# Three head edits in a fused recurrent-scan and gated-MLP kernel: the first loads on one hardware queue, ScalarE copies tile 0's transposes whole, tile 3's statistics ahead of tile 2's norm

## The chip, the cores and the metric

The kernel runs on one core of a Trainium2 chip. The metric is the device time of one execution in microseconds, the median of several runs. A core has five instruction streams that run side by side and meet at semaphores: PE (TensorE, matrix products), DVE (VectorE), ACT (ScalarE), POOL (GpSimd) and SP, which here does nothing but issue DMA transfers. ACT and POOL can issue transfers too; all of them run on the core's 16 DMA engines. Each stream takes its instructions strictly in order.

## The reference

`x` has 2048 rows (tokens) of 448 features. Everything is in bfloat16.

```python
xn = _layernorm(x, axis=-1)                      # (x - mean) / sqrt(var + 1e-5)

# A: a diagonal complex recurrence over the tokens (P = 448 states)
dt = exp(log_dt);  Lam_bar = exp(dt * Lam)
B_bar = ((Lam_bar - 1.0) / Lam)[:, None] * Bmat
Bu = einsum("bld,pd->blp", xn, B_bar)
h_t = Lam_bar * h_(t-1) + Bu_t                   # 2048 steps
s = 2.0 * einsum("blp,dp->bld", hseq, Cmat).real + xn * Dskip

# B: a gated MLP, F = 1792
g = einsum("bsd,df->bsf", xn, w_gate);  u = einsum("bsd,df->bsf", xn, w_up)
g = silu(einsum("bsf,fd->bsd", sigmoid(g) * u, w_down))

return x + s * g
```

## The kernel before, in words

The 2048 rows are 16 tiles of 128 rows; four tiles make a chunk, and four chunks are worked on in turn. For each chunk the normed rows are transposed so that features lie on the partitions (`xnT`, four blocks of 128 features by 512 rows). PE then makes the products with the gate and up weights in seven units each (`g0` to `g6`, `u0` to `u6`, two blocks of 128 outputs per unit), the products with B (`b_phase`), and for an earlier chunk the down product and the product with C. DVE runs the recurrence as a scan after a rotation by tables of sines and cosines (`ssm_pair`, `ssm_stack`), and combines gate and up (`gu_evac`). Chunks 1 to 3 are transposed by DMA; chunk 0 is transposed on PE, since nothing else is there for PE to do.

Products of 448 features are cut into halves of 64 rows, which run beside each other on the two halves of PE's rows: `ph_mm` issues six products of a unit, `z_mm` two more. A unit is `ph_mm`, `z_mm`, `ph_mm`, 14 instructions in 7 pairs.

**The planner.** The code doesn't issue instructions at once. Every operation is added to a plan with its engine, an estimated cost, the keys it reads and writes, and for transfers an assumed landing time (`land=`). `solve` (line 139) computes latest and earliest times and picks an order for each engine; `emit` writes the instructions in that order. PE's order is always that of the program text. DVE's and ACT's order is that of the text while `pl.seq` is true, that is, in the head of the kernel (lines 1094 to 1172); after it the planner is free to choose, so a changed cost or landing time in the head can move DVE and ACT instructions much later in the kernel. Transfers of SP and ACT share eight completion semaphores in turn: the ninth waits for the first to land.

**The head, chunk 0** (lines 388 to 421 and 1093 to 1168). The loads: SP's queue takes x tile 0, x tile 1, the gate weights in six pieces (`load_w`, three blocks of outputs by two halves of the features), x tiles 4 to 7 in two loads, the up weights. ACT's queue takes the row of the recurrence's real parts (`load_p("ACT", 2)`), x tile 2, and x tile 3. POOL's queue takes the two other rows, `log_dt` and the imaginary parts. A first table for ACT's square root is loaded in between.

PE starts with ten products of constants of 512 columns (`warm_mm`). Statistics of tiles 0, 1 and 3 are made on DVE (`bn` then `aggr`), those of tile 2 on ACT (`act_mean`, `act_var`); then a root on ACT (`root`, `act_root`), a reciprocal and the norm on DVE (`recip`, `norm`), in the order of lines 1098 to 1149. Tile 0 is transposed by four 128x128 transposes into two PSUM banks (`pe_transpose`), DVE copies one bank and ACT the other to `xnT`. The three rows of the recurrence are turned into columns by small products in the same place (`columns`; ACT copies them with `copy_pv`). Five more products of constants (`fill`) follow. Tiles 1, 2 and 3 are transposed in eight pieces of 64 rows (`row_transpose`); tile 1's result is copied whole by ACT (`pair_copy`), tiles 2 and 3 in two halves by ACT and DVE (`row_copy`; both halves of tile 3 by DVE).

The gate products of chunk 0 go tile by tile as the tiles arrive: units 0 and 1 of one tile at a time (`units[t]`, 128 columns), unit 2 for two tiles at a time (`pairs`, 256 columns); `front` is a unit's first eight instructions, `back` its last six. The order on PE is: tile 0's transposes, columns, fill, tile 1's transposes, `front` and `back` of `units[0]`, `front` of `units[1]`, tile 2's transposes, `back` of `units[1]`, `front` of `pairs[0]`, `front` of `units[2]`, tile 3's transposes, the rest. The head's last product is followed by unit 3, the first one of 512 columns.

Of the kernel before, what the change touches and what calls it, by code (L numbers as in the profile page):

```python
# [21 lines left out]
P = 128  # L22
# [225 lines left out]
def kernel(  # L248
# [27 lines left out]
    def flat(t, *dims):  # L276
        if len(dims) == 1:
            return t
        names = "abcd"[:len(dims)]
        kw = {n: v for n, v in zip(names[1:], dims[1:])}  # L280
        return t.rearrange("p (" + " ".join(names) + ") -> p " + " ".join(names), **kw)
# [81 lines left out]
    def load_x(t0, n, q="SP", r=(), rate=230e3, land=0.0):  # L363
        load(q, [("x", t) for t in range(t0, t0 + n)], n * P * D * 2,
             x_all[:, t0:t0 + n, :], x_src[:, t0:t0 + n, :], r=r, rate=rate, land=land)
# [3 lines left out]
    def load_w(eng, k, b, part, r=(), land=0.0):  # L369
        m0, m1 = BLK[k][b]  # L370
        c0, c1, r0 = m0 * 2 * P, m1 * 2 * P, (0, 192)[part]
        load(eng, [("w", k, m, part) for m in range(m0, m1)], 4 * P * (c1 - c0), wgt[k][:, 2 * part:2 * part + 2, c0:c1],
             wsrc[k][r0:r0 + 2 * P, c0:c1].rearrange("(s p) f -> p s f", p=P), cost=0.65, r=r, rate=400e3, land=land)
# [17 lines left out]
    def load_p(eng, k, r=()):  # L391
        load(eng, ("vrow", k), D * 2, vrow[k:k + 1, :], (A_log_dt, A_Lambda_im, A_Lambda_re)[k].unsqueeze(0), cost=0.75 if eng == "POOL" else 0.45, r=r)
    load_x(0, 1, "SP")
    load_p("ACT", 2)
    load_x(1, 1, "SP", land=3.6)
    load_x(2, 1, "ACT", land=3.8)
    add("ACT", 0.05, lambda: A.preload_act_table_set("sqrt_and_others"), w=["sqrttab"], lat=1.3, chain=True)
    load_x(3, 1, "ACT", land=4.3)
    load_w("SP", "g", 0, 0, land=5.2)
    load_w("SP", "g", 0, 1, land=5.6)  # L400
    load_p("POOL", 0)
    load_p("POOL", 1)
    add("POOL", 0.15, lambda: G.memset(ident[:], 0.0), w=["ident"], chain=True)
    add("POOL", 0.4, lambda: G.affine_select(out=ident[:], in_=ident[:], compare_op=ALU.not_equal, fill=1.0, base=0,
                                             pattern=[[-1, P]], channel_multiplier=1), r=["ident"], w=["ident"], chain=True)
# [1 line left out]
    load_w("SP", "g", 1, 1, land=7.2)  # L407
    load_w("SP", "g", 2, 0, land=8.4)
    load_w("SP", "g", 2, 1, land=9.6)
    load_x(4, 2, land=10.4)  # L410
    load_x(6, 2, land=11.1)
    add("POOL", 0.1, lambda: G.memset(halfc[:], 0.5), w=["consts"])
    add("POOL", 0.1, lambda: G.memset(negc[:], -1.0), r=["consts"], w=["consts"])
    add("POOL", 0.1, lambda: G.memset(expc[:], math.e), w=["expc"])
# [60 lines left out]
    def act_var(t):  # L475
        add("ACT", 0.7, lambda: A.activation(junk[:], x_all[:, t, :], ACT.Square, bias=nmf[:, t, :], accum_out=sqf[:, t, :]),
            r=[("x", t), ("nf", t)], w=[("mv", t), "junk"])
# [29 lines left out]
    def xkey(t):  # L507
        return t if t < TPC else TPC + t % NXN
# [30 lines left out]
        touch(3)  # L539
        return a  # L540

    def pe_transpose(t, keys, banks):
        o, js = xbuf(t), slice(t * P, t * P + P)
        for i, (key, bank) in enumerate(zip(keys, banks)):
            tp = flat(bank.bitcast(BF16)[:, 0:2 * P], 2, P)

            def f(i=i, tp=tp):
                for s in range(2):
                    T.transpose(tp[:, s, :], o[:, (2 * i + s) * P:(2 * i + s + 1) * P], ident[:, :])  # L549
            add("PE", 0.15, f, r=[("xn", xkey(t)), "ident"], w=[key])  # L550
            eng, cost, e = (("DVE", 0.28, V.tensor_copy), ("ACT", 0.33, A.copy))[i]
            add(eng, cost, lambda e=e, i=i, tp=tp: e(out=xnT[0][:, 2 * i:2 * i + 2, js], in_=tp), r=[key], w=[("xnT", 0, t, i)])

    def pair_copy(t, a, eng):
        js = slice(t * P, t * P + P)
# [547 lines left out]
    aggr(1)  # L1103
    norm(0)
    root(1)
    act_var(2)
    recip(1, 1)
    norm(1)
    uk, ub = [("gu", u2, 0), ("gu", u2, 1)], [gu[u2][:, 0, :], gu[u2][:, 1, :]]
    ak, ab = [("acc", 0), ("acc", 1)], [acc[0][:], acc[1][:]]  # L1110
    units = [[gu_unit(0, "g", m, slots0[m], t, t + 1) for m in range(2)] for t in range(TPC)]
    pairs = [gu_unit(0, "g", 2, u2, t, t + 2) for t in (0, 2)]

    def fill(n):
        def f():
            for _ in range(n):
                T.matmul(gu[slots0[0]][:, 0, 0:P], lhsT=ones[:, 0:P], rhs=ones[:, 0:P], start=True, stop=True)  # L1117
        add("PE", 0.055 * n, f, w=[("gu", slots0[0])])
# [7 lines left out]
        for u in us:  # L1126
            ph_mm(u, 1, stop=stop)

    pe_transpose(0, ak, ab)
    copy_pv = columns(acc[1][:, 400:412], "pvps")  # L1130
    fill(5)
    act_root(2)
    row_transpose(1, uk, ub)
    pair_copy(1, u2, "ACT")
    bn(3)
    recip(2, 1)
    norm(2)
    aggr(3)
    copy_pv()
    add("NONE", 0.0, lambda: None, r=["pv0", ("xn", 0)], w=["pv"], lat=0.0)  # L1140
    front(units[0], True)
    back(units[0])
    front(units[1])
    root(3)
    tp = row_transpose(2, ak, ab)
    for h in range(2):
        row_copy(2, h, ak[h], tp[h])
    recip(3, 1)
    norm(3)
    silu_table()  # L1150
    back(units[1])
    gate(uk, ("gu", u2))
    front(pairs[0:1], True)
    front(units[2])
    tp = row_transpose(3, ak, ab)
    for h in range(2):
        row_copy(3, h, ak[h], tp[h])
    back(units[2])
    back(pairs[0:1])
    turns()  # L1160
    scale(0)
    front(units[3])
    front(pairs[1:])
    back(units[3], True)
    back(pairs[1:], True)
    gu_evac(0, "g", 0, slots0[0])
    gu_evac(0, "g", 1, slots0[1])
    gu_evac(0, "g", 2, slots0[2])
# [113 lines left out]
```

## Time and profile before

| | |
|---|---|
| median of 3 runs | 182.84 us (182.48 to 182.94) |
| the profiled execution's own time | 182.58 us |
| its span in the profile | 180.8 us |
| PE busy in the span | 176.8 us, 98% |
| DVE, ACT, POOL busy | 162.3, 107.2, 26.4 us |
| granted TensorE clock | 1.00 |
| first of tile 0's transposes on PE | 5.32 us |
| first product of the head | 6.47 us |
| first product behind the head (unit 3, 512 columns) | 11.59 us |

Times inside the profile count from the start of the span. A row of the timeline gives the start, the length, the engine (PEld is PE's loading of weights, SPq and ACTq the issuing of transfers), the line of the kernel, the operation, and the tile written and those read (with buffer numbers left out), then how many instructions were merged; in brackets stands how long the engine was idle before and what ended it. Ends of matrix products are modelled, and successive ones overlap, so their starts say more than their lengths. A row of the transfers gives the engine that issued, how many, the size of one, and the median time from issue to landing. A busy engine is not always one that gets on: PE's products in a row that wait for one another in the pipeline count as busy.

### The profile page before, as it was taken

How to read it: one execution, taken by the hardware profiler on the slowest of the kernel's cores; microseconds unless marked ns; L12 is line 12 of the kernel's file. 1: busy time of each engine (PE TensorE's matmuls, PEld its weight loads, DVE VectorE, ACT ScalarE, POOL GpSimd, SP SyncE). 2: the span in 40 equal slices, each digit the busy share in tenths (PEclk: the TensorE clock that was granted, in tenths of full speed). 3: DMA queues.
4: the chain of work that ended last, by engine and by line, in shares of the span. 5: the costliest groups of instructions: out<-in, count | busy, mean ns of one | idle time of the engine just before them, and what ended most of it. 6: DMA issues, size and time to landing. Idle time of an engine off the chain costs nothing.

```text
span 180.8 us, 3804 instructions
## 1 busy us (share of the span) xinstructions
PE 176.8 (98%) x1507; PEld 89.5 (49%) x1507; DVE 162.3 (90%) x300; ACT 107.2 (59%) x175; POOL 26.4 (15%) x76
## 2 busy tenths in 40 slices
PE   8999999999999999999999999999999999999993
PEld 2775555564544444445554444454554444455552
DVE  2776899999997889999999998999999999999572
ACT  3889992966698898473265333599221599711100
POOL 5374224000028118600000000000000000000000
DMA  5999833998000320000032000000000000012131
GB/s 151 370 362 243 127 60 63 300 235 231 1 0 0 62 58 0 4 0 0 4 62 56 0 4 0 0 29 25 25 2 4 0 0 0 4 51 75 54 119 39
DMA packets 23941, 12.73 MB, mean 70 GB/s; under 512 B 14833, under 2 KB 23922, under 8 KB 23922
## 3 DMA queue, kind: packets, MB, share of 16 engines
q1 hardware_dynamic: 23568, 12.24, 26.9%
q8 instruction: 12, 0.20, 0.5%
q10 hardware_dynamic: 290, 0.23, 0.4%
q14 instruction: 7, 0.06, 0.1%
q0 software_dynamic: 64, 0.00, 0.0%
HBM read 7.23 MB, written 1.84 MB: 50 GB/s over the span
## 4 chain that ended last, share of the span: by engine, by line
PE 95%; DMA 2%; DVE 1%; SPq 0%; issue 0%; DVEq 0%
PE gu L798 42%; PE gu L1015 15%; PE acc L1034 10%; PE acc L1015 9%; PE acc L798 9%; PE gu L788 7%; DMA x_all<-in_A_x_dram 2%; PE gu L1034 1%; PE acc L788 1%; DVE o_t L1076 0%; DVE bst L433 0%; DVE o_t L1070 0%; PE acc L549 0%; SPq L360 0%; PE gu L1117 0%; DVE g_t L519 0%
## 5 line engine op out<-in xcount | busy, mean ns | idle before, releaser
L798 PE MATMUL gu<-xnT,wU 64*128 64x512 bf16 x288 | 41.8, 376 | 0.0
L798 PE MATMUL gu<-xnT,wG 64*128 64x512 bf16 (+2 forms) x348 | 37.9, 325 | 0.0
L1015 PEld LDWEIGHTS <-hF 128*128 128x128 bf16 x224 | 21.7, 98 | 21.2 <-issue 1.3
L1015 PE MATMUL gu<-wd,hF 128*128 128x448 bf16 x140 | 28.0, 352 | 0.0
L798 PEld LDWEIGHTS <-wG 64*128 64x128 bf16 x420 | 19.2, 94 | 17.2 <-issue 0.2
L798 PEld LDWEIGHTS <-wU 64*128 64x128 bf16 x336 | 17.0, 94 | 18.6 <-PE gu L798 0.2
L954 DVE TENSOR_TENSOR_SCAN wv<-c_r,st,z 128x512 bf16<-128x512 f32 x18 | 22.9, 1277 | 0.0
L1021 ACT ACTIVATE g_t<-gu 128x448 bf16<-128x448 f32 x10 | 5.4, 543 | 28.8 <-PE gu L1015 28.7
L853 ACT ACTIVATE sig<-gu 128x1024 f32<-128x1024 f32 x16 | 16.3, 1022 | 9.5 <-PE gu L798 9.3
L1034 PE MATMUL acc<-cT,hT 128*128 128x448 bf16 (+2 forms) x105 | 20.0, 335 | 0.0
L798 PE MATMUL gu<-xnT,bT 64*128 64x512 bf16 x144 | 19.3, 376 | 0.0
L861 DVE SCALAR_TENSOR_TENSOR hF<-sig,gu 128x1024 bf16<-128x1024 f32 x13 | 15.8, 1218 | 2.2 <-PE gu L798 2.0
L1015 PE MATMUL acc<-wd,hF 128*128 128x448 bf16 x84 | 16.9, 353 | 0.0
L1034 PEld LDWEIGHTS <-hT 128*128 128x128 bf16 x126 | 11.7, 98 | 9.9 <-issue 0.4
L904 ACT CAST bus<-gu 128x1024 bf16<-128x1024 f32 x12 | 11.9, 1013 | 6.9 <-PE gu L798 6.6
L798 PEld LDWEIGHTS <-bT 64*128 64x128 bf16 x192 | 9.7, 94 | 8.8 <-issue 1.1
L798 PE MATMUL acc<-xnT,wG 64*128 64x512 bf16 x72 | 10.6, 376 | 0.0
L910 ACT CAST bus<-acc 64x256 bf16<-64x256 f32 (+1 forms) x24 | 8.6, 369 | 2.7 <-PE acc L798 2.5
L788 PE MATMUL gu<-xnT,wG 64*128 64x512 bf16 (+2 forms) x58 | 9.6, 325 | 0.0
L853 ACT ACTIVATE sig<-acc 128x512 f32<-128x512 f32 x10 | 5.6, 592 | 6.6 <-PE acc L798 6.6
L433 DVE BATCH_NORM_STATS2 bst<-x_all 128x6 f32<-128x448 bf16 x11 | 6.5, 615 | 3.3 <-DMA x_all<-in_A_x_dram 3.3
L788 PE MATMUL gu<-xnT,wU 64*128 64x512 bf16 x48 | 9.2, 376 | 0.0
(161 smaller groups left out, 271.2 us busy)
## 6 DMA issues: line engine op xcount, KB each, us to landing
wd<-in_B_w_down_dram SPq DMA_DIRECT2D x2, 784.0 KB, 5.9
x_all<-in_A_x_dram SPq DMA_DIRECT2D x6, 224.0 KB, 4.1
wG<-in_B_w_gate_dram SPq DMA_DIRECT2D x4, 256.0 KB, 4.1
wU<-in_B_w_up_dram SPq DMA_DIRECT2D x4, 256.0 KB, 6.2
out_dram<-o_t SPq DMA_DIRECT2D x8, 112.0 KB, 1.7
wG<-in_B_w_gate_dram SPq DMA_DIRECT2D x2, 384.0 KB, 5.7
wU<-in_B_w_up_dram SPq DMA_DIRECT2D x2, 384.0 KB, 6.9
out_dram<-ctmp SPq DMA_DIRECT2D x6, 112.0 KB, 1.7
```

Of the source, the lines that this page charges most:

```text
L433: add("DVE", 0.56 if t < TPC else 0.6, lambda: V.bn_stats(out=bst[b][:], in_=x_all[:, t, :]), r=[("x", t)] + ([("xnT", 0, 3, 1)] if 3 < t ...
L788: row_mm(banks[b], b, lambda: T.matmul(out[b], lhsT=w(b, hs, s), rhs=x(b, hs, s), start=start, stop=False), start)
L798: row_mm(banks[b], h, lambda: T.matmul(out[b], lhsT=w(b, hs, ss[q]), rhs=x(b, hs, ss[q]), start=start and q == 0, stop=stop and q == 2), s ...
L853: add("ACT", act(n), lambda s=s, src=src: A.activation(th[:, s, :], src, ACT.Tanh, scale=0.5), r=keys, w=[tk])
L861: add("DVE", dve1(n), lambda s=s, src=src: V.scalar_tensor_tensor(out=ho[:, s, :], in0=th[:, s, :], scalar=1.0, in1=src, op0=ALU.add, op1= ...
L904: add("ACT", act(1024), lambda: A.copy(out=bus[u][:], in_=gu[slots[pt]][:]), r=key(pt), w=[("bus", u)])
L910: add("ACT", 0.36, lambda ns=ns, d=d, q=q, l=l, i=i: A.copy(out=bus[u][d, l, ns], in_=acc[a3[i]][q, 0:256]), r=[("acc", a3[i])] + ([("bus" ...
L954: dve(1.194, lambda k=k: V.tensor_tensor_scan(out=wv[:, k, :], data0=rb, data1=z[:, k, :], initial=(st[pt][:, k, :] if c else 0.0), op0=AL ...
L1015: T.matmul(d, lhsT=hF[c % 2][:, m, h, js], rhs=wd[:, ft, :], start=(ft == 0), stop=(ft == FT - 1))
L1021: add("ACT", act(448), lambda: A.activation(g_t[g][:], d, ACT.Silu, scale=0.5), r=[key, "silutab"], w=[("gt", g)])
L1034: T.matmul(y, lhsT=hT[c % 2][:, hm, js], rhs=cT[:, cm, c0:c1], start=(i == 0 and not skip_on_pe), stop=(i == 6))
```

## The change

Five things are edited, all in the head:

- x tile 2 and x tile 3 move from ACT's queue to SP's. SP now issues x tiles 0, 1, 2, the first two pieces of the gate weights, x tile 3, and then the other pieces. ACT's queue gets the row of imaginary parts that POOL issued. x tiles 4 to 7 become one load. The assumed landing times are set anew.
- Tile 0's four transposes go into one bank, and ACT copies it whole, ahead of the square of tile 2 (`act_var(2)` moves behind it). Tile 1's whole copy moves from ACT to DVE. The fill is four products, not five.
- On DVE, tile 3's aggregate stands ahead of tile 2's reciprocal and norm, and tile 3's reciprocal and norm directly behind; its root on ACT moves up too.
- On PE, both `back` of `units[1]` and the first six products of `pairs[0]` stand ahead of tile 2's transposes; the rest of `pairs[0]` ahead of tile 3's, and these ahead of `front` of `units[2]`. Transposes of tiles 2 and 3 go to different columns of the two `acc` banks. The waits as built still go by bank: tile 3's transposes wait for ACT's and DVE's copies of tile 2.
- `back` of `units[3]` stands ahead of `front` of `pairs[1]`.

The number of gate products is the same. On PE the order of everything behind the head is unchanged; on DVE and ACT the planner's order changes in many places behind the head.

```diff
     load_x(0, 1, "SP")
     load_p("ACT", 2)
-    load_x(1, 1, "SP", land=3.6)
-    load_x(2, 1, "ACT", land=3.8)
+    load_p("ACT", 1)
+    load_x(1, 1, "SP", land=3.3)
+    load_x(2, 1, "SP", land=3.9)
     add("ACT", 0.05, lambda: A.preload_act_table_set("sqrt_and_others"), w=["sqrttab"], lat=1.3, chain=True)
-    load_x(3, 1, "ACT", land=4.3)
-    load_w("SP", "g", 0, 0, land=5.2)
-    load_w("SP", "g", 0, 1, land=5.6)
+    load_w("SP", "g", 0, 0, land=4.9)
+    load_w("SP", "g", 0, 1, land=5.8)
+    load_x(3, 1, "SP", land=6.2)
     load_p("POOL", 0)
-    load_p("POOL", 1)
...
-    load_x(4, 2, land=10.4)
-    load_x(6, 2, land=11.1)
+    load_x(4, 4, land=11.1)
...
-    def pe_transpose(t, keys, banks):
+    def pe_transpose(t, key, bank):
         o, js = xbuf(t), slice(t * P, t * P + P)
-        for i, (key, bank) in enumerate(zip(keys, banks)):
-            tp = flat(bank.bitcast(BF16)[:, 0:2 * P], 2, P)
-
-            def f(i=i, tp=tp):
-                for s in range(2):
-                    T.transpose(tp[:, s, :], o[:, (2 * i + s) * P:(2 * i + s + 1) * P], ident[:, :])
-            add("PE", 0.15, f, r=[("xn", xkey(t)), "ident"], w=[key])
-            eng, cost, e = (("DVE", 0.28, V.tensor_copy), ("ACT", 0.33, A.copy))[i]
-            add(eng, cost, lambda e=e, i=i, tp=tp: e(out=xnT[0][:, 2 * i:2 * i + 2, js], in_=tp), r=[key], w=[("xnT", 0, t, i)])
+        tp = flat(bank.bitcast(BF16)[:, 0:4 * P], 4, P)
+
+        def f():
+            for s in range(4):
+                T.transpose(tp[:, s, :], o[:, s * P:s * P + P], ident[:, :])
+        add("PE", 0.3, f, r=[("xn", xkey(t)), "ident"], w=[key])
+        add("ACT", 0.57, lambda: A.copy(out=xnT[0][:, :, js], in_=tp), r=[key], w=[("xnT", 0, t, 0), ("xnT", 0, t, 1)])
...
     root(1)
-    act_var(2)
     recip(1, 1)
...
-    pe_transpose(0, ak, ab)
+    def to_acc(t):
+        c0 = (t - 2) * P
+        keys = [("tp", t, i) for i in range(2)]
+        return keys, row_transpose(t, keys, [a[:, c0:c0 + P] for a in acc])
+
+    pe_transpose(0, "tp0", acc[0][:])
     copy_pv = columns(acc[1][:, 400:412], "pvps")
-    fill(5)
+    fill(4)
+    act_var(2)
     act_root(2)
     row_transpose(1, uk, ub)
-    pair_copy(1, u2, "ACT")
+    pair_copy(1, u2, "DVE")
     bn(3)
-    recip(2, 1)
-    norm(2)
     aggr(3)
     copy_pv()
...
+    root(3)
+    recip(2, 1)
+    norm(2)
+    recip(3, 1)
+    norm(3)
     front(units[0], True)
     back(units[0])
     front(units[1])
-    root(3)
-    tp = row_transpose(2, ak, ab)
-    for h in range(2):
-        row_copy(2, h, ak[h], tp[h])
-    recip(3, 1)
-    norm(3)
-    silu_table()
     back(units[1])
     gate(uk, ("gu", u2))
-    front(pairs[0:1], True)
+    ph_mm(pairs[0], 0, start=True)
+    k2, tp2 = to_acc(2)
+    for h in range(2):
+        row_copy(2, h, k2[h], tp2[h])
+    z_mm(pairs[0], False)
+    back(pairs[0:1])
+    k3, tp3 = to_acc(3)
+    for h in range(2):
+        row_copy(3, h, k3[h], tp3[h])
+    silu_table()
     front(units[2])
-    tp = row_transpose(3, ak, ab)
-    for h in range(2):
-        row_copy(3, h, ak[h], tp[h])
     back(units[2])
-    back(pairs[0:1])
     turns()
     scale(0)
     front(units[3])
+    back(units[3], True)
     front(pairs[1:])
-    back(units[3], True)
     back(pairs[1:], True)
+    gate(["tp0", "pvps", *k2, *k3], [("acc", 0), ("acc", 1)])
```

More of the change, by code (lines that the diff above doesn't have):

```diff
@@ L1109 @@
     uk, ub = [("gu", u2, 0), ("gu", u2, 1)], [gu[u2][:, 0, :], gu[u2][:, 1, :]]
-    ak, ab = [("acc", 0), ("acc", 1)], [acc[0][:], acc[1][:]]
     units = [[gu_unit(0, "g", m, slots0[m], t, t + 1) for m in range(2)] for t in range(TPC)]
```

## The prediction

> **What bounds the kernel now.** I read the page first, then the chain of waits, then the timeline of the first 12 us, since the edits lie there. The page, busy time and slices:
>
> ```profile
> span 180.8 us, 3804 instructions
> PE 176.8 (98%) x1507; PEld 89.5 (49%) x1507; DVE 162.3 (90%) x300; ACT 107.2 (59%) x175; POOL 26.4 (15%) x76
> PE   8999999999999999999999999999999999999993
> ```
>
> PE is the bound from its first slice to its last; the chain of waits gives it 95% of the span. A stage that merely has less to wait for is worth nothing unless PE's own stream starts earlier or loses a hole. The chain of the first 13 us, in order of time (start, length, what):
>
> ```profile
> 1.18 2.91 DMA x_all<-in_A_x_dram
> 4.12 0.63 DVE bst L433
> ...
> 4.97 0.31 DVE g_t L519
> ...
> 5.32 0.42 PE acc L549 x4
> ...
> 6.02 0.39 PE gu L1117 x5
> 6.41 0.22 PE gu L568 x8
> ```
>
> The head hangs on x tile 1. It lands at 1.18 + 2.91 = 4.09; its statistics stand on DVE ahead of tile 0's reciprocal and norm; then PE works without a hole: transposes of tile 0, the columns, five fills, transposes of tile 1, products. The timeline of that stretch (start, length, engine, line):
>
> ```profile
> 5.32 0.42 PE L549 MATMUL acc<-ident,g_t 128*128 128x128 bf16 x4
> ...
> 6.34 0.29 PE L568 MATMUL gu<-ident,g_t 64*128 64x64 bf16 x8
> ...
> 6.47 0.33 PE L798 MATMUL gu<-xnT,wG 64*128 64x128 bf16 x6
> ...
> 6.67 0.58 ACT L558 COPY xnT<-gu 128x512 bf16<-128x512 bf16 x1
> ...
> 7.79 0.28 PE L568 MATMUL acc<-ident,g_t 64*128 64x64 bf16 x8
> ...
> 8.20 0.29 DVE L575 COPY xnT<-acc 128x256 bf16<-128x256 bf16 x1 [0.84 <-PE acc L568]
> ...
> 9.12 0.28 PE L568 MATMUL acc<-ident,g_t 64*128 64x64 bf16 x8
> ...
> 9.50 0.49 DVE L575 COPY xnT<-acc 128x256 bf16<-128x256 bf16 x2 [0.49 <-PE acc L568]
> ...
> 11.59 0.40 PE L788 MATMUL acc<-xnT,wG 64*128 64x512 bf16 x2
> ```
>
> Products start at 6.47 and the head's last one gives way at 11.59: 5.12 us. Products of the two row halves run in pairs: 56 pairs of 128 columns at 0.056 and 14 of 256 at 0.11 make 4.66, two transpose groups at 0.12 make 4.9. So only about 0.2 us of it is waiting, 0.14 of that for tile 3's copies (DVE to 9.99). The DMA rows that matter:
>
> ```profile
> x_all<-in_A_x_dram SPq DMA_DIRECT2D x2, 112.0 KB, 2.5
> x_all<-in_A_x_dram ACTq DMA_DIRECT2D x2, 112.0 KB, 3.3
> wG<-in_B_w_gate_dram SPq DMA_DIRECT2D x4, 256.0 KB, 4.1
> ```
>
> The sum is made against the profiled execution: 182.58 us, span 180.8. It lies 0.26 under the median of 182.84, to which I add the difference. A measurement here can tell about 0.3%, 0.55 us.
>
> **Start of the transposes.** x2 and x3 leave ACT's queue, so x1 shares the DMA engines with nothing large. Bounds for its landing: x0's 2.1 us from issue (3.3) and today's 2.9 (4.09). Nearest row: the sharing ones show 2.9 to 3.6, the unshared one 2.1, so about 3.5. The Trainium skill, "DMA: Bandwidth & Descriptors", section "Issuing engines are not separate DMA queues", says that transfers issued from several engines interleave on the same DMA engines and only issue time is saved. The trace agrees (2.1 alone, 2.9 and 3.0 shared); if the queues were independent, x1 would stay at 4.09, which is a rival below. DVE can take x1's statistics 0.12 after the aggregate of 3.54, at 3.7 instead of 4.12: norm 0 ends at 4.84 instead of 5.26. PE then has its ten warm-up products in the way: weight loads every 0.43, the last at 4.13 one product ahead, so the tenth runs from 4.56 to 4.98. Transposes start at 4.98, not 5.32: 0.34 gained.
>
> **Start of the products.** From there to the transposes of tile 1 PE needed 6.34 - 5.32 = 1.02; one fill less takes 0.06 off: 5.94. Tile 1's norm is ready: ACT's mean of x2 begins when the root of 4.13 is done (x2, now third on SP's queue, has today's 4.28 and x1's 3.5 as bounds, 3.9 in the middle), so root and norm 1 come 0.17 earlier and end at 5.77. The whole copy on ACT starts after the transposes, 5.40, now ahead of the square of tile 2 that held it until 6.06; it takes the 0.58 of the 128x512 copy: 6.03. Products start 0.13 after 5.94, at 6.07: **0.40 gained**, and DVE's half copy (0.28) is off the path. Weights: w1 of block 0 is issued at 2.12, about 4.0 to landing, 6.1. By then x2 and x3 had crossed too; in the new order x3 comes behind it, so 5.8; even at 6.1 it costs under 0.05. The imaginary row moves from POOL's queue (2.03 + 3.5 = 5.5, which would be late for columns at 5.33) to ACT's second issue (1.28; at most the 3.0 that x2 takes from there today, 4.3).
>
> **The DVE chain that PE meets next.** Tile 1's pair copy goes from ACT to DVE. No row shows a 128x512 copy from PSUM there; two 128x256 ones take 0.49, a two-input operation on 512 columns 0.68. A copy is nearest the former: 0.52. It starts 0.1 after the group's end (8.07 to 8.20, 9.41 to 9.50), at 5.94 + 0.29 + 0.1 = 6.33. Then in order: x3's statistics (6.78; overlap of 0.07 as at 6.06), aggregate +0.66 (7.44), reciprocal +0.11, norm 2 +0.20 = 7.75, ending 8.16; tile 2's transposes at 8.22. Today x3's aggregate came behind norm 2. PE arrives after two tiles of products and 6 of 256 columns (today 6.47 to 8.56, less a transpose group's 0.11: 1.98), at 8.05: **a new wait of 0.17**. Behind the blocked transposes stand all later products. Then 0.11 and eight 256-column products, 0.44: PE at tile 3's transposes at 8.77. These write the banks of tile 2's copies and so wait for ACT's and DVE's. DVE does norm 3 first (8.28, +0.33), then its copy 8.61 to 8.90: start 8.95, **0.18 of new wait**. The rest: 0.12 + 0.78 + 0.78 + 0.78 = 2.46, and about 0.04 for tile 3's second copy: 11.45 against 11.59.
>
> **Costed at nothing.** One load of x4 to x7 delays their statistics from 10.88 to about 11.3 (5.2 + 6.1); DVE's idle 1.9 us in 12 to 20 us covers it; without that, 0.4. ACT's table load slips from 8.49 to about 9.0 and the first scale ends near 11.0, before the first evacuation of 11.31; past that, every 0.1 is 0.1 for ACT. Root of x3: ready near 8.0, asked for at 8.1. POOL issues one DMA less, 0.51, before work not needed until 4.98. SP issues x2 and x3 in addition, 0.4 each, ahead of weights that wait for bandwidth.
>
> **Sum:** -0.40 + 0.17 + 0.18 + 0.04 - 0.14 (old wait gone) = about -0.15. Carried to the end, as PE shows no hole behind: 182.84 - 0.15 = 182.7 us.
>
> **The rivals.**
> - *Front gains nothing.* x1 stays at 4.09, or PE's clock is still low. Warm-ups run at 0.43 per 512 columns, the fills of 5.95 already at 0.06 per 128, so the rate doubles between 4.56 and 5.4. Were it low until 5.4, transposes cost 0.05 more each and products start some 0.2 later. Without the front's gain the DVE chain remains: +0.2, 183.0. The granted clock of 1.00 throughout says nothing on it. The Trainium skill, "TensorE: Matmul & The Clock Gate", Part 1, puts the change around 4 us into sustained activity, give or take 0.5 us, here 4.3 to 5.3: that speaks against starting transposes at 4.98, and by it alone the time would be up to 0.2 above the sum, 182.9.
> - *Slower: x3 holds DVE.* x3 is now sixth on SP's queue and its statistics stand ahead of norm 2, norm 3 and two copies. Needed at 6.78. For 6.2: the bytes ahead of it are those that were across when w1 landed at 6.1. Against: w1 of today plus one more tile; the next load in line took 4.4, to 7.0. Each 0.1 past 6.78 is 0.1; it is slower than before from 6.93, at 7.0 +0.1 (182.9), and reaches 0.3% only at 7.5 (183.4).
> - *Slower: the written order of DVE shifts later too.* In the first scan stage one more scan (1.14) stands before the first up-product of chunk 1, against a 0.3 and two 0.2 operations moved ahead: 39.04 + 0.75 + 1.21 = 41.0, where PE refills that bank at 41.18. Slack 0.9 becomes 0.2. A few such places missed by 0.3 to 0.6 give 183.3 to 183.7. Against: PE waits nowhere today.
> - *Faster by more.* Both new waits fall away (shorter copy, earlier norm): products from 6.07 end 4.98 later at 11.05, -0.54: 182.3, just at the limit.
>
> **How the numbers follow.** Forecast (-0.4 to +0.1) 0.55; front without gain 0.15; x3 late 0.08; DVE order 0.12; faster by more 0.10, all of it counted as faster although its time lies at the limit. Within 0.55 us stay the forecast, the front without gain, three quarters of x3's case (it must pass 7.5) and a sixth of the DVE order's: 0.55 + 0.15 + 0.06 + 0.02 = 0.78. Slower: 0.02 + 0.10 = 0.12. Faster: 0.10. The forecast's own range is 182.4 to 182.9. The full range takes in the fifth case, with 0.3 below it because runs of one kernel already spread over 0.46 (182.48 to 182.94), and the DVE order above: 182.0 to 183.7.
>
> **What would show it.** x1's statistics near 3.7; transposes of tile 0 near 5.0; products near 6.1; a wait of PE's weight loads on tile 2's norm near 8.2 and on DVE's copy near 8.95; the first acc product (11.59 today) near 11.45, and an equal lead afterwards. Wrong if transposes start at 5.3, if x3's statistics wait for DMA after 6.8, or if PE has holes after 12 us.

## The result, and the profile after

The change makes the kernel slower by 0.8 us: 183.70 us median of 6 runs (183.54 to 183.94) against 182.89 us (182.48 to 183.15), a ratio of 1.0046 with a 95% interval of 1.0033 to 1.0060. Run again later beside other kernels it gave 183.93 against 182.79, 1.0066 (1.0053 to 1.0078). The forecast was 182.7, no change that can be told. The profiled execution took 183.77 us, 1.19 more than that of before.

The page of the changed kernel, span, busy times, PE's slices, and one group of instructions (its last columns are busy time, mean ns, idle time before them and what ended most of it):

```profile
span 182.0 us, 3796 instructions
PE 177.8 (98%) x1506; PEld 87.7 (48%) x1506; DVE 162.9 (89%) x300; ACT 106.4 (58%) x174; POOL 26.7 (15%) x75
PE   8999999999999999999999999999999999999993
L795 PEld LDWEIGHTS <-wG 64*128 64x128 bf16 x420 | 18.3, 94 | 18.8 <-PE gu L785 0.6
```

PE is busy from end to end as before, and its busy time has grown by 1.0 us for one product fewer: waiting inside PE's pipeline counts as busy, so the shares tell nothing here. The last column does: 0.6 us in which weight loads waited for PE's own line 785, `z_mm`. Before, the same group has 0.2 there, for issue. The chain of waits of the first 14 us (start, length, what):

```profile
2.60 0.47 SPq L360
...
4.09 4.80 DMA wG<-in_B_w_gate_dram
...
8.95 0.31 PE gu L795 x3
...
9.62 0.50 PE gu L795 x6
...
12.46 0.50 PE gu L795 x6
```

The head used to hang on x tile 1. Now it hangs on the second half of the weights' second block, issued by SP at 4.09 and landed 4.80 later, at 8.89; before, the last of the 16 engines was done with it at 8.08 (14 of them by 7.40), 0.27 before PE wanted it at 8.35. The 7.4 and 7.7 that expectations below name leave the last engines out in the same way. PE's part of the timeline (start, length, line, operation, tiles, how many):

```profile
4.99 0.63 PE L547 MATMUL acc<-ident,g_t 128*128 128x128 bf16 x4
...
5.86 0.61 PE L1112 MATMUL gu<-const-bfloat16-1.0 128*128 128x128 bf16 x4
6.40 0.40 PE L565 MATMUL gu<-ident,g_t 64*128 64x64 bf16 x8
6.60 0.36 PE L795 MATMUL gu<-xnT,wG 64*128 64x128 bf16 x6
...
7.09 0.75 PE L795 MATMUL gu<-xnT,wG 64*128 64x128 bf16 x18
7.67 0.22 PE L785 MATMUL gu<-xnT,wG 64*128 64x128 bf16 x2
...
8.95 0.39 PE L795 MATMUL gu<-xnT,wG 64*128 64x256 bf16 x3 [0.21 <-DMA wG<-in_B_w_gate_dram]
...
9.62 0.50 PE L795 MATMUL gu<-xnT,wG 64*128 64x256 bf16 x6
9.96 0.28 PE L565 MATMUL acc<-ident,g_t 64*128 64x64 bf16 x8
...
12.13 0.27 PE L785 MATMUL gu<-xnT,wG 64*128 64x256 bf16 x2
12.46 0.50 PE L795 MATMUL gu<-xnT,wG 64*128 64x256 bf16 x6
12.80 0.38 PE L785 MATMUL acc<-xnT,wG 64*128 64x512 bf16 x2
```

Tile 0's transposes start at 4.99, a third of a microsecond earlier, as forecast; but they take 0.63 instead of 0.42, the fills 0.61, and the products start at 6.60 instead of 6.47. Unit 3 starts at 12.80 instead of 11.59. The weight loads of that stretch that waited longest (in brackets the idle time and what ended it):

```profile
8.94 0.11 PEld L795 LDWEIGHTS <-wG 64*128 64x128 bf16 x3 [0.49 <-DMA wG<-in_B_w_gate_dram]
9.62 0.22 PEld L795 LDWEIGHTS <-wG 64*128 64x128 bf16 x6 [0.26 <-PE gu L785]
12.46 0.22 PEld L795 LDWEIGHTS <-wG 64*128 64x128 bf16 x6 [0.34 <-PE gu L785]
```

Behind unit 3 no time is won or lost. The last group of products of the kernel starts, before and after, at

```profile
177.34 0.37 PE L1034 MATMUL acc<-cT,hT 128*128 128x64 bf16 x7
```

```profile
178.53 0.37 PE L1031 MATMUL acc<-cT,hT 128*128 128x64 bf16 x7
```

which is 165.75 and 165.73 after unit 3. In all 20 profiles of this study the kernel's time was the start of unit 3 plus 171.0 to 171.3, but for one (below). So the time is read off one number, the start of unit 3; it is made of the products' start and what lies between. From start to start, the 1.21 us between 11.59 and 12.80 are: products 0.13 later; a product of the late weights 0.478 behind its partner on the other 64 rows (8.47 to 8.95), where 0.003 is normal, +0.48; the steps from 9.29 and 12.13 0.331 and 0.335 instead of 0.106, +0.45; and a smaller loss that shows only when rows are counted out. The 18 instructions at 7.09 are nine pairs. They take 7.67 - 7.09 = 0.58, nine clean pairs of 0.056 would take 0.50. Such a stretch with 0.08 too much stands in the old order once (tile 0) and in the new one four times: +0.25. The old wait for tile 3's copies is gone, -0.14. Sum 1.17; the other 0.04 lies in steps of a few hundredths. In the kernel before, the z products of unit 2's second pair are followed by tile 3's last products, and the step there is the normal one:

```profile
10.82 0.29 PE L788 MATMUL gu<-xnT,wG 64*128 64x256 bf16 x2
10.93 0.84 PE L798 MATMUL gu<-xnT,wG 64*128 64x128 bf16 x18
```

### The profile page after: what moved, and what is told of

The parts are those of the page before. It is cut to its first block, busy times and chain, and to the rows that moved or that the text cites. A ratio compares the mean times of both kernels' runs of the same rounds, so it can differ in the third digit from the quotient of the medians.

```text
span 182.0 us, 3796 instructions
## 1 busy us (share of the span) xinstructions
PE 177.8 (98%) x1506; PEld 87.7 (48%) x1506; DVE 162.9 (89%) x300; ACT 106.4 (58%) x174; POOL 26.7 (15%) x75
## 3 DMA queue, kind: packets, MB, share of 16 engines
HBM read 7.23 MB, written 1.84 MB: 50 GB/s over the span
## 4 chain that ended last, share of the span: by engine, by line
PE 93%; DMA 3%; SPq 2%; DVE 1%; issue 0%; DVEq 0%
PE gu L795 41%; PE gu L1012 15%; PE acc L1031 10%; PE acc L1012 9%; PE acc L795 9%; PE gu L785 7%; DMA wG<-in_B_w_gate_dram 3%; SPq L360 2%; PE gu L1031 1%; PE acc L785 1%; DVE o_t L1073 0%; DVE o_t L1067 0%; PE acc L565 0%; PE acc L1029 0%; DVEq L1073 0%
## 5 line engine op out<-in xcount | busy, mean ns | idle before, releaser
L795 PEld LDWEIGHTS <-wG 64*128 64x128 bf16 x420 | 18.3, 94 | 18.8 <-PE gu L785 0.6
L795 PEld LDWEIGHTS <-wU 64*128 64x128 bf16 x336 | 16.3, 94 | 19.2 <-PE gu L795 0.2
L795 PEld LDWEIGHTS <-bT 64*128 64x128 bf16 x192 | 9.1, 94 | 9.4 <-issue 1.1
```

The costliest lines, as they stand in the source:

```text
L795: row_mm(banks[b], h, lambda: T.matmul(out[b], lhsT=w(b, hs, ss[q]), rhs=x(b, hs, ss[q]), start=start and q == 0, stop=stop and q == 2), s ...
```

## The experiments

The theory from these two profiles had two parts. **S**: PE waits for its own products. `row_mm` (lines 770 to 778) lets a product wait for the last one that the other 64 rows wrote to the same bank. A unit's last six products write the banks that its first eight wrote from the other rows. In the old order other work stands between them nearly everywhere; in the new order `back` follows `front` or `z_mm` directly (called a meeting below), so that the product to be waited for has only just started. **L**: the new loads bring x tile 3 and the weights late. The rivals: that one of the two is all, that what shows is chance of one execution, or that something behind the head costs time. Every time below is a median of 5 to 12 runs beside runs of the kernel before on the same chip, whose median was 182.61 to 182.81.

**The new code with the old loads.**

```diff
+    load_x(2, 1, "ACT", land=3.8)      # and x tile 3, the row on POOL, tiles 4-5 and 6-7: as before
-    load_x(2, 1, "SP", land=3.9)
```

> The changed kernel with the loads of before: x tiles 2 and 3 and one row on the queues where they were, x tiles 4 to 7 in two loads; PE, ACT and DVE of the head as changed. In the changed kernel unit 3 starts at 12.79 us instead of 11.59, and the second half of the weights' block 1 lands at 8.89 instead of about 7.4. Theory L (the loads cost most): that half lands near 7.4 again, PE's gap of 0.48 at 8.46 is gone, products start near 6.5, the two waits for the other rows' product in a pair's bank (0.22 each) stay; unit 3 near 12.3, the time near 183.2 to 183.3. Rival C (the code's order costs nearly all): unit 3 stays near 12.7 and the time within 0.15 of 183.7.

Measured 183.26, ratio 1.0024 (0.9997 to 1.0051), half of the loss. No weight is late. The second half of the block landed at 8.10, much as before (8.08). But PE's two waits are there, unchanged (PE's timeline):

```profile
9.24 0.27 PE L786 MATMUL gu<-xnT,wG 64*128 64x256 bf16 x2
9.58 0.50 PE L796 MATMUL gu<-xnT,wG 64*128 64x256 bf16 x6
9.92 0.28 PE L566 MATMUL acc<-ident,g_t 64*128 64x64 bf16 x8
...
12.09 0.27 PE L786 MATMUL gu<-xnT,wG 64*128 64x256 bf16 x2
12.42 0.50 PE L796 MATMUL gu<-xnT,wG 64*128 64x256 bf16 x6
12.76 0.38 PE L786 MATMUL acc<-xnT,wG 64*128 64x512 bf16 x2
```

The step from 12.09 to 12.42 is 0.33 where 0.106 is normal, and that from 9.24 to 9.58 likewise. From the products' start (7.08 here, because the imaginary row came late on POOL's queue and the columns waited 0.73 for it) to unit 3 it is 5.68 against 5.12 before, 0.56 more: 0.46 + 0.25 - 0.14 = 0.57. **S** accounts for all of it.

**The old code with the new loads.** The five load lines of the change, nothing else.

> The kernel before with only the changed loads. Theory L: the second half of block 1 lands near 8.9 here too, PE waits for it where unit 2's first products stand, 0.3 to 0.7; x tile 1 lands near 3.2 and the products still start near 6.5, since PE's clock is not up earlier; unit 3 at 12.0 to 12.3, the time 183.2 to 183.5. Rival C (loads innocent): unit 3 at 11.2 to 11.6, the time 182.5 to 182.9.

Measured 183.63, 1.0052 (1.0035 to 1.0068): the loads alone cost as much as the whole change. The mechanism is not the one expected. Weights were not the last wait; x tile 3 was. A row of DVE's timeline and one of PE's:

```profile
7.26 0.63 DVE L432 BATCH_NORM_STATS2 bst<-x_all 128x6 f32<-128x448 bf16 x1 [1.63 <-DMA x_all<-in_A_x_dram]
```

```profile
8.46 0.29 PE L567 MATMUL acc<-ident,g_t 64*128 64x64 bf16 x8 [1.10 <-DVE g_t L518]
```

In the old order too, tile 3's statistics stand ahead of tile 2's norm; x tile 3 lands at 7.23, DVE idles 1.63 us for it, and PE 1.10 for the norm. Products had started at 5.88, early, and the gain was lost.

**Which of the loads.** Three kernels move one tile, each from the changed kernel, PE's and DVE's orders kept.

```diff
-    load_x(3, 1, "SP", land=6.2)
+    load_x(3, 1, "ACT", land=4.3)      # first kernel: x tile 3 on ACT's queue
```

> The changed kernel with x tile 3 alone moved back to ACT's queue, behind the two rows and the table; the order of PE and DVE is unchanged. Theory X (a tile of x among the weights on one queue slows what comes behind it): x tile 3 lands near 5.3, the second half of block 1 near 7.5 to 7.9, PE's wait on it (0.37 above its normal step) is gone; unit 3 near 12.4, the time near 183.3. Rival Q (the one load of x tiles 4 to 7, or the single queue, slows it): the half still lands at 8.5 or later, unit 3 near 12.8, the time near 183.7.

```diff
-    load_x(2, 1, "SP", land=3.9)
+    load_x(2, 1, "ACT", land=3.9)      # second: x tile 2 on ACT's queue
```

> The changed kernel with x tile 2 alone moved back to ACT's queue; x tile 3 stays on SP's, behind the first weights; PE and DVE in the same order. Theory X (x tile 3 among the weights is enough): x tile 3 lands at 7 or later, the second half of block 1 at 8.5 or later, unit 3 at 12.5 or later, 183.5 or more. Rival T (it takes x tile 2 on SP's queue as well, or alone, since moving x tile 3 away did not help): 350 GB/s or more from 4.5 us on, x tile 3 lands near 6.2, the second half of block 1 by 7.9, unit 3 near 12.2, the time 183.0 to 183.3.

```diff
+    load_x(3, 1, "SP", land=4.5)       # third: x tile 3 ahead of the first weights
     load_w("SP", "g", 0, 0, land=4.9)
```

> The changed kernel with x tile 3 issued on SP's queue ahead of the first weights, so that no tile of x stands among them; nothing else is moved. Theory X (a tile of x among the weights slows the queue, and the late tile holds DVE): x tile 3 lands near 4.7, 350 GB/s or more from 4.5 us on, first weights near 5.6 and 6.5, the second half of block 1 by 8.0, unit 3 near 12.2, the time 183.0 to 183.3. Rival Q (all of it on one queue is what slows it): under 300 GB/s somewhere between 4.5 and 7 us, the second piece of the first weights at 7 or later, so that products wait for it, unit 3 at 12.6 or later, the time 183.5 or more.

Measured 183.48, 183.37 and 183.74 (1.0041, 1.0029, 1.0061); none restores the loads. The half of the block landed at 8.5, 8.69 and 8.46. In the first the first weights were late instead, a step of 0.94 on PE; in the second PE's products came 0.98 late by the two halves together; in the third, where x tile 3 landed at 4.32 and no longer held DVE, 0.37. A tile among the weights is thus not the cause by itself.

**The split, and the row.**

```diff
-    load_x(4, 4, land=11.1)
+    load_x(4, 2, land=10.4)            # first: x tiles 4 to 7 in two loads again
+    load_x(6, 2, land=11.1)
```

> The changed kernel with x tiles 4 to 7 in two loads again and nothing else. Theory Q (the tiles of x on SP's queue slow the weights; the slow stretch began at 5.1, before the one load was issued at 5.63): the DMA engines again move under 300 GB/s somewhere between 4.5 and 7 us, x tile 3 lands at 7 or later, the time within 0.15 of 183.7. Rival (the one load of four tiles slows the rest): 350 GB/s or more from 4.5 us on, x tile 3 near 6.2, the second half of block 1 by 7.9, the time 183.3 or less.

```diff
-    load_p("ACT", 1)
+    load_p("POOL", 1)                  # second: the imaginary row back on POOL's queue
```

> The changed kernel with only the imaginary row back on POOL's queue. Theory R: x tile 3 lands near 6.2, the second half of block 1 by 8.0, the DMA engines move 350 GB/s from 4.5 us on; the time 183.2 to 183.4, for the meetings on PE stay. Rival X: under 300 GB/s somewhere between 4.5 and 7 us, x tile 3 at 6.8 or later, the half at 8.4 or later; the time within 0.15 of the changed kernel on the same chip. If the row lands after 5.6, PE's columns wait for it and add that much.

> The changed kernel as it is, on the chip of the other three runs: what they are compared with, and another look at its landings and at PE's clock. 183.6 to 184.0; x tile 3 at 6.8 or later, the second half of block 1 at 8.4 or later, two gaps of 0.33 on PE at unit 2's pairs.

Measured 184.01, 184.12 and, for the changed kernel itself, 183.93. Neither edit helps; x tile 3 landed at 7.09, 7.16 and 7.62. Theory R, the row, falls for the changed kernel. In the kernel before the row alone was moved, and then the two tiles of x alone:

```diff
+    load_p("ACT", 1)
     load_x(1, 1, "SP", land=3.6)
-    load_p("POOL", 1)
```

> The kernel before with the imaginary row as ACT's second issue instead of POOL's, nothing else; PE's and DVE's orders are the same. In the runs so far the second half of block 1 landed at 8.3 to 9.3 wherever that row was on ACT's queue, with x on either queue, and at 7.4 and 7.7 in two of three with it on POOL's. Theory R (that row's place makes the weights late): the half after 8.2, PE waits for it, the time 183.1 or more with single runs spread over 0.8. Rival X (it is the tiles of x on SP's queue, the others were chance): the half by 7.8, the time 182.6 to 182.9.

```diff
-    load_x(2, 1, "ACT", land=3.8)
+    load_x(2, 1, "SP", land=3.8)       # x tile 3 likewise, behind the first weights
```

> The kernel before with x tiles 2 and 3 on SP's queue at the places that the change gives them, nothing else; the two rows stay on ACT's and POOL's queues, x tiles 4 to 7 in two loads; PE's and DVE's orders are the same. Theory X (tiles of x on SP's queue make the loads late): under 300 GB/s somewhere between 4.5 and 7 us, x tile 3 at 6.8 or later; its statistics hold tile 2's norm and PE waits for that at tile 2's transposes, 0.5 to 1.1; unit 3 at 12.1 to 12.5, the time 183.3 to 183.7. Rival (it takes all the edits to the loads together): x tile 3 by 6.4, the time 182.7 to 182.95.

The row: 182.95, 1.0014 (1.0004 to 1.0024), a small loss and not by late weights: x tile 2, now behind the row, landed at 4.70 (4.27 before), and ACT's root for tile 1 stood behind its mean. The two tiles: 183.13, 1.0024 (1.0011 to 1.0037), 0.5 above the kernel before on that chip, the low end of what theory X expected, with single runs in two groups, five from 182.62 to 182.82 and seven from 183.10 to 183.76 us. The profiled one was of the first group. x tile 3 landed at 6.08 in it, DVE waited 0.38 for it and had the time, and PE lost nothing; yet the DMA engines were slow there too. The last column is GB/s, the one before it the engines' busy share, per half microsecond, first the kernel before:

```profile
5.50:6.00 0.50, 0.50 (x10) 0.36 (x9) 0.47 (x2) 0.45 (x2) 0.00 (x0) 1.00 1.07 375
6.00:6.50 0.50, 0.50 (x17) 0.39 (x17) 0.50 (x2) 0.44 (x2) 0.00 (x0) 1.00 1.13 383
```

then the kernel before with the two tiles on SP's queue:

```profile
5.50:6.00 0.50, 0.50 (x9) 0.43 (x8) 0.23 (x1) 0.03 (x1) 0.00 (x0) 1.00 0.93 244
6.00:6.50 0.50, 0.50 (x9) 0.36 (x9) 0.39 (x1) 0.50 (x2) 0.00 (x0) 1.00 0.91 219
```

and the changed kernel:

```profile
5.50:6.00 0.50, 0.50 (x9) 0.42 (x8) 0.00 (x0) 0.35 (x1) 0.00 (x0) 1.00 0.94 249
6.00:6.50 0.50, 0.50 (x9) 0.30 (x9) 0.00 (x0) 0.50 (x2) 0.00 (x0) 1.00 0.80 250
```

Over all 20 profiles, means from 5 to 7 us: 225 to 325 GB/s in the eleven kernels with x tile 2 or 3 on SP's queue, 305 to 374 in the nine with both on ACT's (four of these under 340, among them all but one of those with the row on ACT's queue). So the place of the tiles lowers the rate, though the two groups overlap between 305 and 325, and whether that costs time is decided by when x tile 3 and the block's second half happen to be complete: x tile 3 behind the first weights came at 6.1 to 7.9, where 6.1 was in time, and the half of the block, with the changed kernel's code, at 8.5 to 9.3, where it was wanted at about 8.5 at the latest. Late weights are not peculiar to the new loads: of those nine profiles, four have PE waiting 0.4 to 1.1 us for them, one of the five with the old order on PE and three of the four with the new or a mixed one.

**The waits on PE alone.** The change's last line was moved in the kernel before, and moved back in the changed one:

```diff
-    front(pairs[1:])
     back(units[3], True)
+    front(pairs[1:])
     back(pairs[1:], True)
```

> The kernel before with one line moved and nothing else: the last six products of each unit of tile 3 ahead of the first eight of unit 2's second pair, as in the change. No load, no statistic and no transpose moves. Theory S (a unit's last six products write the banks that its own first eight wrote from the other rows, and PE waits for its own pipeline when nothing stands between): about 0.23 for unit 2's pair and 0.07 for the units of tile 3, so unit 3 0.30 later for the same start of products, the time 183.05 to 183.1 against 182.76. Rival (the gaps in the changed kernel are of the loads or of DVE): no gap there, the time within 0.1 of the kernel before.

> The changed kernel with that same line moved back and nothing else. Its head up to tile 3's transposes is that of the changed kernel, so it is also a second look at that kernel's landings and at PE's clock. Theory S: PE's gap of 0.335 at the last pair becomes its normal 0.106, unit 3 0.30 earlier for the same landings, the time near 183.4 against 183.70. Rival: within 0.1 of 183.7.

In the kernel before: 183.10 against 182.76, 1.0030 (1.0003 to 1.0057), +0.34 for one line that moves no load, no copy and no norm. The wait it makes (PE's timeline; this profiled execution was one of the slowest of its twelve, 183.99, with late weights as well, which have no part in this row):

```profile
12.35 0.27 PE L788 MATMUL gu<-xnT,wG 64*128 64x256 bf16 x2
12.69 0.50 PE L798 MATMUL gu<-xnT,wG 64*128 64x256 bf16 x6
13.02 0.38 PE L788 MATMUL acc<-xnT,wG 64*128 64x512 bf16 x2
```

In the changed kernel the step is 0.106 again when the line is moved back, and the median 183.65 beside 184.01 of the kernel with the split loads in the same set of runs; that is hardly below 183.70, so this run by itself does not show the 0.30. Its profile has products at 5.89 and a wait of 1.4 for the weights: the gain was taken by the next wait.

**Both meetings of unit 2 apart**, first with the new loads, then with the old ones and the row on ACT's queue, where the third kernel is what the fourth is compared with:

```diff
-    back(pairs[0:1])
     k3, tp3 = to_acc(3)                # tile 3's transposes and copies
+    back(pairs[0:1])
```

> The changed kernel with unit 2's last six products no longer directly behind its two z products: tile 3's transposes stand between them for the first pair, the last six of the units of tile 3 for the second, as before the change. Theory S (each such meeting makes PE wait about 0.22 for its own product): both waits go, unit 3 near 12.35, the time near 183.3; PE's wait on the second half of block 1 stays. Rival (the 0.22 is filling that the next wait takes over, tile 3's transposes or the copies behind them): unit 3 moves by under 0.15, the time stays within 0.15 of 183.7.

> The changed kernel's code with the loads of before but for one row: x tiles 2 and 3 on ACT's queue, x tiles 4 to 7 in two loads, and the imaginary row as ACT's second issue, as in the change, so that PE's columns do not wait for POOL's queue. The four profiles so far give time = start of unit 3 + 171.0. Theory L (the order of x on one queue slows the loads, the row does not): the DMA engines move 350 to 390 GB/s from 4.5 us on, products start at 6.1 to 6.5, the two waits for the other rows' product stay, unit 3 at 11.8 to 12.1, the time 182.8 to 183.1. Rival R (the row on ACT's queue slows the loads): under 300 GB/s somewhere between 4.5 and 7 us, the second half of block 1 after 8.4, the time 183.4 or more.

> The code and loads of the run with the row on ACT's queue, and besides unit 2's last six products apart from its z products, as in the earlier run of that edit. Theory S (two waits of 0.22 go once no load is late): unit 3 at 11.3 to 11.7, the time 182.3 to 182.7, 0.3 to 0.45 below the run without this edit and at or below the kernel before. Rival (the waits turn into others, for ACT's and DVE's copies of tile 2 ahead of tile 3's transposes): within 0.15 of the run without this edit.

Measured 183.95, 183.48 and 183.44 (1.0060, 1.0039, 1.0030). At the last pair the wait went. At the first pair it turned into the one that the rival named. Tile 3's transposes now stand directly behind the z products and wait for ACT's copy of tile 2 (PE's timeline of the kernel with the old loads):

```profile
9.31 0.29 PE L566 MATMUL acc<-ident,g_t 64*128 64x64 bf16 x8 [0.33 <-ACT xnT L573]
```

So the new order loses there either way: tile 2's copies are done about 0.6 after its last transpose (8.71 to 9.31 here), and a pair's last products, 0.32, fill only half of that. In the kernel with the row on ACT's queue the DMA engines moved 336 to 379 GB/s from 5 to 7 us, as expected, and still the block's second half landed at 9.11: its first engine was done at 7.09, its last two microseconds later. That loss is not explained by the rate, and the time, 183.48, lies above what theory L gave.

**The best of both, tried.**

```diff
-    ph_mm(pairs[0], 0, start=True)
+    front(pairs[0:1], True)
     k2, tp2 = to_acc(2)
-    z_mm(pairs[0], False)
     back(pairs[0:1])                   # with the old loads, the row as ACT's last, the last line as before
```

> The changed kernel's code with three things undone: x tiles 2 and 3 on ACT's queue and x tiles 4 to 7 in two loads, as before; the imaginary row as ACT's last issue, not POOL's; on PE the first eight products of unit 2's first pair stand together ahead of tile 2's transposes and the last six behind them, and the last line is back as before. If the meetings on PE and the loads are the whole loss: products start at 6.0 to 6.5, one gap of about 0.22 stays behind tile 2's transposes instead of two of 0.335, unit 3 5.3 to 5.4 behind the products' start, at 11.4 to 11.9, the time 182.4 to 182.9. If something else of the change costs time as well: 183.2 or more with no late weight in the profile.

Measured 183.16, 1.0020 (0.9999 to 1.0041): 0.5 to 0.8 better than the change, not better than before. Products start at 5.96, but the fourth pair waits 0.97 for weights that landed at 6.98; without that it would be 5.49 to unit 3, 0.1 more than expected. An earlier start of the products runs into the first weights.

**A wait of the kernel before, taken away.** The change replaced the 0.14 that PE lost on tile 3's copies. What that is worth alone:

```diff
-(("ACT", 0.33, A.copy), ("DVE", 0.25, V.tensor_copy))[h or t == 3]
+(("ACT", 0.33, A.copy), ("DVE", 0.25, V.tensor_copy))[h]
-    silu_table()                       # moved behind tile 3's copies
```

> The kernel before with one of its own waits taken away: ACT makes the first half of tile 3's copy, ahead of its table load, so that the two halves run side by side instead of one after the other on DVE; PE's order is the same. PE's gap of 0.25 at 9.79 (0.14 above its step) should go and nothing be late behind it: the time 182.6 to 182.65. Rival: ACT's table load, some 1.3 us later than before, holds its first evacuations (the first is at 11.31 now): 182.8 to 183.2.

Measured 183.18, 1.0021 (1.0011 to 1.0032): slower. The wait is gone, the products take 4.98 to unit 3 instead of 5.12. But ACT's table load starts at 10.06 instead of 8.49, its first evacuation at 11.98 instead of 11.31, and unit 4 waits for it (PE's timeline):

```profile
11.68 0.38 PE L788 MATMUL acc<-xnT,wG 64*128 64x512 bf16 x2
11.90 0.81 PE L798 MATMUL acc<-xnT,wG 64*128 64x512 bf16 x6
13.04 0.39 PE L788 MATMUL gu<-xnT,wG 64*128 64x512 bf16 x2 [0.33 <-ACT hF L853]
```

This is the one profile with a loss behind unit 3, 0.5 us. The change has nearly as late a table load (9.86); PE is later there too, so that nothing waits for it.

**The smaller meeting.**

```diff
-    back(units[0])
     front(units[1])
+    back(units[0])
```

> The kernel before with tile 0's last products behind tile 1's first ones, so that its one meeting on PE (0.075 in its profile) goes; nothing else is moved. Theory S: the steps of 0.058 to 0.098 at tile 0's last products become 0.056, unit 3 0.07 earlier for the same start, the time 0.05 to 0.1 below the kernel before. Rival (a product waits there for the other rows' product whatever stands between): the long steps stay, no change.

Measured 183.24, 1.0034 (1.0021 to 1.0047). The edit does not do what it was meant to. Tile 1's products write the same banks from the same rows as tile 0's, so the last products of tile 0 still follow such a product directly and the long steps stay, as the rival says; and tile 1's first products now stand where tile 1's copy isn't ready, 0.39 lost. What it shows is that the meeting belongs to the bank, not to the unit; the size of the small ones, 0.08, rests on the counted rows alone.

## Why the prediction was wrong

**What held.** x tile 1 landed at 3.2 (3.5 forecast), its statistics began at 3.62 (3.7), tile 0's transposes at 4.99 (4.98, behind the ten warm-ups as said). The planner's new order of DVE behind the head cost nothing: 165.75 and 165.73 from unit 3 to the end. The copy of tile 1 on DVE took 0.42 (0.52).

**Start of the products, 0.40 gained: mis-sized, and the rival without gain was right in this profile.** The step from transposes to products assumed PE at full rate. In 11 of the 20 profiles tile 0's four transposes took 0.61 to 0.63, in nine 0.39 to 0.42. The kernel with x tile 3 on ACT's queue has the changed kernel's PE instructions one for one, and shows

```profile
4.91 0.39 PE L547 MATMUL acc<-ident,g_t 128*128 128x128 bf16 x4
```

where the changed kernel has 4.99 and 0.63. In five profiles with the changed head the products started at 5.89 to 6.60, 6.28 in the mean, and in four with the old head and the old loads at 6.47, 6.48, 6.70 and 6.74, 6.60: about 0.3 was gained on average, nothing in the execution first profiled. The Trainium skill, "TensorE: Matmul & The Clock Gate", Part 1, says that the window behind the gate is free-running, so that the moment of the change varies from run to run of one kernel; the forecast drew on that section for the moment only, 4.3 to 5.3 on this trace. The 20 profiles agree that the moment varies, and by more than that: in one of them the warm-up products stand 0.22 apart, not 0.43, from 3.63 on, and in others the rate doubled only near 6.6.

**The DVE chain that PE meets next, its products at full rate: the step that failed.** "The rest: 0.12 + 0.78 + 0.78 + 0.78 = 2.46" counts products at their rate and puts PE's wait for its own products at nothing; so does "eight 256-column products, 0.44" ahead of it. From tile 3's transposes to unit 3 it took 12.80 - 9.96 = 2.84, with old loads also 2.84; the first meeting of unit 2, 0.23, lies in the eight products. Between the two transposes the forecast had a wait of 0.18 for copies; PE's wait for its own z products stood there first and hid it. The order of `z_mm` and `back` and the wait in `row_mm` were in the code that was read; that two that follow each other directly differ from two with something between was not seen. The kernel before had shown it in one place, tile 0, as nine pairs in 0.59. The Trainium skill, "TensorE: Matmul & The Clock Gate", section "Single matmul latency", gives (398 + N) / 2.4 ns for one product over 128 rows (those here have 64), 272 for 256 columns, against a step of about 109 in a stream; an estimate by it is 0.16 for each of the two meetings, where 0.23 was measured. It agrees in kind: the step is that of a product which waits for the end of the one before.

**Costed at nothing: the weights behind x.** "SP issues x2 and x3 in addition ... ahead of weights that wait for bandwidth" assumed that the same bytes cross in the same time. They did not: 294, 249, 250, 250 GB/s from 5 to 7 us where 354 to 383 went across before. The weights' second block was complete at 8.89, needed at 8.47: +0.48, and 0.4 to 1.5, counted alike, in four other profiles of kernels with these first loads and this code. The second rival, x tile 3 late, was right in its place and its size: it landed at 7.26, not 6.2, and tile 2's norm ended at 8.63, not 8.16; in the changed kernel PE stood at the weights until 8.95, so it didn't decide, and with the old code it did (1.10).

**Costed at nothing: ACT's table load.** It cost nothing in the profile, but that says little: it started at 9.86, not 9.0, because tile 2's copy on ACT came late, and PE was later still. With PE on time a load at 10.06 cost 0.5, as the run with tile 3's copy on ACT shows; whether one at 9.0 would have been early enough for the chain to 11.45, no run shows.

**The sum.** Forecast -0.40 + 0.17 + 0.18 + 0.04 - 0.14 = -0.15. By the runs it is about -0.3 + 0.45 + 0.25 - 0.14 and 0.4 to 1.5 for late weights, +0.7 to +1.8; measured +0.8 and +1.1. The new code alone cost +0.45 and the new loads alone +0.82, 1.27 added up, which the two together do not quite reach. A likely reason, not tested, is that a wait which PE serves at one place need not be served at the next.

**What stays open.** Why the DMA engines are slower with x tiles 2 or 3 on SP's queue is not settled. In the changed kernel single 896-byte packets took up to 1436 ns, where most take 41, and the engines' busy share fell to 0.76; in the kernel before with the two tiles on SP's queue the rate fell as far with no packet of that size over 335 ns. Of the edits to the loads, taken apart, only the place of the tiles moves the rate that far; how it does is not shown, and the move changes the order and the time of issue as well (x tile 3 at 3.12 instead of 1.71), so that queue and order are not told apart. The Trainium skill, "DMA: Bandwidth & Descriptors", "Issuing engines are not separate DMA queues", says that the choice of the issuing engine saves only issue time. By itself that does not explain what was measured here, 374 GB/s and 278 for the same bytes and the same code.

## What to carry to other kernels

Before moving instructions on an engine that is never idle, list for each what it waits for on its own engine, and what stood between the two: a product that follows directly on one that it must wait for cost 0.08 to 0.23 us here, and busy shares hide it. Time gained at a start is worth only what the next resource has ready, so carry the earlier time through each later stage, down to the weights and the evacuations, before counting it. Where landings and the clock's change move by a microsecond or more from one execution to the next, take several profiles of a kernel before calling one of its waits the cause.

## What the runs showed of the hardware

- Where two tiles were loaded changed the total rate: between 5 and 7 us the kernel before moved 374 GB/s with x tiles 2 and 3 on ACT's queue and 278 with them on SP's, one behind the first weights, and nothing else edited; 358 and 261 with the changed kernel's code, where the other loads differ too.
- A load is complete when its slowest engine is. The 16 engines ended one 256 KB load between 7.05 and 8.08 in the kernel before, between 7.24 and 8.89 in the changed one, and between 7.09 and 9.11 in a kernel whose mean rate was undisturbed.
- PE's rate doubled at times spread over some 3 us, from about 3.6 to about 6.6. Up to 4.5 us all these programs give PE the same ten products.
